# Squares of one gate group moved to the last quarter of the first gate/value phase

## The chip, the cores and the metric

The kernel runs on one core of one Trainium2 chip. The metric is the device time of one execution in microseconds, as the median of several runs. Its engines are TensorE (PE, with its weight loads as PEld), VectorE (DVE), ScalarE (ACT), GpSimd (POOL) and SyncE (SP). In this kernel SP only issues transfers; POOL issues transfers and a few small operations.

## The reference

A complex gated recurrence feeds a gated feed-forward block with a residual.

```
mag  = sqrt(a_re^2 + a_im^2);  scale = min(mag, 0.999) / (mag + 1e-6)
a    = (a_re + i a_im) * scale                       # 4 x 8 heads, 768 steps, 48 wide
S_t  = a_t * S_(t-1) + k_t v_t^T                     # complex state, real input
y_t  = q_t . Re(S_t)
x    = y as [3072 tokens, 384]
out  = x + sigmoid(x @ w_res) * ((gelu(x @ w_gate) * (x @ w_val)) @ w_out)
```

The widths are 384 for the model and 1536 for the feed-forward block.

## The kernel before, in words

**Groups and units.** The 768 steps of each of the four batches are cut in three stretches of 256. A batch and a stretch make a *group*: 256 tokens with all eight heads, held as two halves of 128 tokens on the partitions. There are 12 groups, ordered by stretch first. Groups are put together in *units*: group 0 alone, then 1 and 2, 3 and 4, 5 and 6, and so on, group 11 alone. So the fourth unit holds groups 5 and 6, and its first group is group 5. Group 6 is called `HELD`, and its squares are placed elsewhere in the program.

**How the recurrence becomes products.** For each group the log of the squared magnitude, `lm`, is summed along the tokens by products with a triangular matrix (`cs_l`, L272), and so is the angle `th` (`cs_t`, L291, reduced to a fraction of a turn on DVE in L295 and L296, with its absolute value in L301). Exponentials of the sums (`E`, `Ei`) and sines (`CS`) scale q and k (`products`, L369 to L381) into `padQ` and `padK`. Within a half the output is a masked score product times v; between halves and groups a decayed state `G` is carried. From group 3 on the transposed `QT` and `KT` come from a DMA transpose that SP issues (L385); the score products that read them are at L446. In earlier groups PE transposes (L459, L462) and ACT and DVE copy the result (`qk`, L464 and L465).

**The squares.** `squares(g)` gives three steps. `q0` (L217) squares `ar` on ACT into `lm`. `q1` squares `ai` on ACT into `sq` (L231; on DVE for groups 1 to 4). `q2` (L235) adds the two on DVE with a ceiling, and for groups 3 to 5 issues the decay transfers of that row on POOL (`decay_raw`, L333, then L316). The first two are allowed to go to the queue only after the last gelu issued so far (`paced("gelu")`), the third only after the last gelu product (`paced("gmul")`).

**Phases.** After a ramp, each unit `u` has a phase y (gate, value, gelu, their product, residual gate) and each following unit a phase x (logs, exponentials, angles, sines, and the output product of the unit before). Phase y of unit `u` takes in the first half of the attention of unit `u + 1`, the products of q and k for it, and the squares of a later unit. In phase y of unit 0 those are the three steps of group 5 alone. The gate/value work is twelve `gv_step`s (PE at L595 and L599, gelu on ACT, the product with the value on DVE at L602) and two residual gates (`rp_step`, PE at L611, a tanh on ACT, called `sg`). Their results share four PSUM banks with the transposes of x (`xt_step`, L580), so a product can wait for the bank that an earlier one frees. All calls of ACT's helper `act` show as L144; a change of ACT's function table is L639.

**What sets the order.** `weave` spreads the steps of each stream evenly between a begin and an end, and runs them in order of that place. A planner then puts the instructions of each engine in a queue; helpers such as `paced` and `tab` tie some of them down. [...] SP's queue holds the loads of `ar`, `ai`, `q` and `k` (L164, L172), the outputs (L626), one decay row per group (L349) and the DMA transposes (L385). POOL's queue holds the loads of v, the weights, the small decay transfers and the adding of residuals; a load of v waits on POOL until the `k` of the same group has landed (L201).

Of the kernel before, what the change touches and what calls it, by code (L numbers as in the profile page):

```python
# [17 lines left out]
def weave(*streams):  # L18

    order = []  # L20
    for si, (begin, end, steps) in enumerate(streams):
        n = len(steps)
        for i, step in enumerate(steps):
            order.append((begin + (end - begin) * (i + 0.5) / n, si, i, step))
    for _, _, _, step in sorted(order, key=lambda e: e[:3]):
        step()
# [3 lines left out]
def kernel(  # L30
# [36 lines left out]
    LATE0, LATE1 = 0.6, 1.0  # L67
# [141 lines left out]
    def paced(nm):  # L209
        return tc.issue_after(T[nm].ins) if nm in T else nullcontext()  # L210

    def squares(g):

        def q0():
            T["lm", g] = pS.tile([128, W], FP, tag="s", name="lm")
            with paced("gelu"):
                nc.scalar.activation(out=T["lm", g], in_=flat(T["ar", g]), func=AF.Square)  # L217

        def q1():
            if g < 5:  # L220
                if g == 0:
                    T["sq"] = hb.tile([128, 4, 2, DM], FP, tag="h2", name="sq0")
                t = T["sq"][:, g % 4].rearrange("p a m -> p (a m)")
            else:
                t = pE.tile([128, W], FP, tag="E", name="sq")
            T["sq", g] = t
            if g in DVSQ:
                nc.vector.tensor_tensor(out=t, in0=flat(T["ai", g]), in1=flat(T["ai", g]), op=OP.mult)
            else:
                with paced("gelu"):  # L230
                    nc.scalar.activation(out=t, in_=flat(T["ai", g]), func=AF.Square)  # L231

        def q2():
            with paced("gmul"):
                nc.vector._custom_dve(TENSOR_ADD_SAT, out=T["lm", g], in0=T["lm", g], in1=T["sq", g], s0=MAG2MAX, s1=0.0)  # L235
            if g in LATER and g != HELD:
                decay_raw(g)
        return [q0, q1, q2]
# [127 lines left out]
    def products(g):  # L366
        def x0():
            qE = flat(T["q", g]).bitcast(BF)[:, 0:W]
            nc.vector.tensor_tensor(out=qE, in0=flat(T["q", g]), in1=T["E", g], op=OP.mult)  # L369
            T["qE", g] = qE  # L370

        def x1():
            kE = flat(T["k", g]).bitcast(BF)[:, 0:W]
            nc.vector.tensor_tensor(out=kE, in0=flat(T["k", g]), in1=T["Ei", g], op=OP.mult)
            T["kE", g] = kE

        def mk(nm, src):
            def x():
                t = pads[nm, g % 2][:, :, 0:DD].rearrange("p x (u d) -> p x u d", u=2)
                sb = T[src, g].rearrange("p (x u d) -> p x u d", u=1, d=D).to_broadcast([128, C * H, 2, D])  # L380
                nc.vector.tensor_tensor(out=t, in0=T["CS", g], in1=sb, op=OP.mult)  # L381
                T[nm, g] = t
                if g >= TURN:
                    tt = trp.tile([128, C * H, 128], BF, tag=nm + "T", name=nm + "T")
                    T["turn"] = nc.sync.dma_start_transpose(out=tt, in_=pads[nm, g % 2])  # L385
                    T[nm + "T", g] = tt
            return x
        return [x0, mk("Q", "qE"), x1, mk("K", "kE")]
# [248 lines left out]
    def table(nm):  # L637
        def f():
            tab(nc.scalar.preload_act_table_set(nm))  # L639
        return f  # L640

    def gs(u):
        return UNITS[u] if 0 <= u < NU else []
# [7 lines left out]
    def call(f, *a):  # L651
        return lambda: f(*a)
# [4 lines left out]
    def att_steps(u, half):  # L657

        todo = [(g, c, i * C + c) for i, g in enumerate(gs(u)) for c in range(C)]
        n = len(todo) // 2  # L660
        steps = []
        for i, (g, c, jj) in enumerate(todo[half * n:half * n + n]):
            steps += attention(g, c)
            if i > 0:
                steps.insert(-1, call(xt_step, u, jj - 1))
        if n:
            steps.append(call(xt_step, u, half * n + n - 1))
        return steps
# [109 lines left out]
    def phase_y(u):  # L778

        gv = []  # L780
        if 0 <= u < NU:
            table("gelu_and_others")()
            gv = [call(gv_step, u, f) for f in range(KF)]
            rp = [call(rp_step, u, jj) for jj in range(len(gs(u)) * C)]
            gv = gv[:8] + rp[:len(rp) // 2] + gv[8:] + rp[len(rp) // 2:]
        def late(nm, f):
            with paced(nm):
                f()
        dec3 = [call(decay3, g) for g in gs(u + 1)]
        sq = [f for w in range(NU) if P1AT.get(w, w - 2) == u + 1 for g in gs(w) if g != HELD for f in squares(g)]  # L790
        pr = [(0.0, 0.4, [st for g in gs(u + 1) for st in products(g)])]
        if u == 0:
            g1, g2 = gs(1)
            pr = [(0.0, 0.15, [call(late, "last", f) for f in products(g1)]),
                  (0.35, 0.6, [call(late, "gmul", f) for f in products(g2)])]
        weave((0.0, 1.0, gv), *pr, (0.55, 0.56, dec3), (0.5, 0.95, sq), (0.3, 0.95, att_steps(u + 1, 0)) if u < 1 else (LATE0, LATE1, att_steps(u + 1, 0)))

    for g in range(3):
        load_a(g)
# [11 lines left out]
    for u in range(NU + 1):  # L811
        if u > 0:
            phase_x(u)
        if u == 1:
            with paced("turned"):
                decay_raw(HELD)
        residuals()
        phase_y(u)
        for g in gs(u + 2):
            with paced("turn"):  # L820
                load_q(g)
            after_landing(T["k", g], call(load_v, g))
        while T["a"] < min(NG, gs(u + 1)[-1] + 7 if gs(u + 1) else NG):
            with paced("turn"):
                load_a(T["a"])
# [30 lines left out]
```

## Time and profile before

| what | value |
|---|---|
| runs shown, median of 5 | 290.3 us (289.24 to 291.03) |
| profiled execution, time | 290.88 us |
| its span, first to last instruction | 288.9 us |
| granted TensorE clock, mean | 0.959 |
| PE busy | 244.5 us (85%) |
| DVE busy | 216.2 us (75%) |
| ACT busy | 198.4 us (69%) |
| POOL busy | 93.3 us (32%) |
| bytes moved | 44.01 MB, mean 152 GB/s |
| packets under 512 B | 165092 of 176001 |

The span is what the profile's views cover; the time of an execution has about 2 us more. Busy shares are means over the whole span: the phases differ in what limits them. Phase y of unit 0 covers about 43 to 68 us, phase x of unit 1 from there to about 91 us, and phase y of unit 1 from there to about 110 us, by the places of the table loads and gelus in the timeline of ACT.

### The profile page before, as it was taken

Reading aid. Unit: us, or ns where it says so; the run is one execution under the profiler, and the core shown is the slowest. Engines: PE = TensorE matmul, PEld = TensorE weight load, DVE = VectorE, ACT = ScalarE, POOL = GpSimd, SP = SyncE. Lnnn points to the kernel's source line nnn. Section 1 sums busy time; section 2 is a strip of 40 time slices with the busy share of each in tenths; the row PEclk is TensorE's granted clock in tenths of the full one; section 3 lists DMA queues with packets and bytes.
Section 4 is the critical chain, followed back from the end, with each engine's and each line's share of the span. In section 5 each row is a group of like instructions: output and inputs, shape, how many; then the busy total and the mean of one; then the engine's idle time right before and its main releaser. Section 6 shows DMA issues by size and latency. Waiting matters only on the chain.

```text
span 288.9 us, 5120 instructions
## 1 busy us (share of the span) xinstructions
PE 244.5 (85%) x1835; PEld 148.2 (51%) x1848; DVE 216.2 (75%) x376; ACT 198.4 (69%) x336; POOL 93.3 (32%) x141
## 2 busy tenths in 40 slices
PE   0445758866986998999999999989999998999994
PEld 0122437755653455554566554556545665455782
DVE  0679996945599986899796998869977577564553
ACT  4876996458798579995689975787565746455250
POOL 4021851130352602467304492124821242100220
PEclk9968987977899999999999999999999999999999
DMA  8999999899999999969999979997499566900631
GB/s 144 187 175 186 172 200 193 151 177 194 161 178 214 163 195 173 176 141 184 178 203 168 148 130 205 191 173 64 75 216 219 87 59 133 189 16 23 141 56 56
DMA packets 176001, 44.01 MB, mean 152 GB/s; under 512 B 165092, under 2 KB 175976, under 8 KB 175976
## 3 DMA queue, kind: packets, MB, share of 16 engines
q1 hardware_dynamic: 140744, 33.05, 67.1%
q0 software_dynamic: 35232, 10.64, 36.2%
q8 instruction: 14, 0.23, 0.3%
q14 instruction: 11, 0.09, 0.1%
HBM read 31.33 MB, written 9.08 MB: 140 GB/s over the span
## 4 chain that ended last, share of the span: by engine, by line
PE 61%; ACT 17%; DVE 8%; DMA 6%; issue 4%; SPq 3%; POOL 0%; DVEq 0%; ACTq 0%
PE vp L599 15%; PE gp L595 15%; PE op L619 12%; PE cst L291 4%; PE csl L272 3%; PE rp L611 3%; ACT L639 3%; DMA k<-in_k_dram 3%; ACT CS L144 2%; PE at L446 2%; ACT lm L144 2%; ACT ar L144 2%; DMA d<-lm 2%; SPq L172 2%; PE dk L488 2%
## 5 line engine op out<-in xcount | busy, mean ns | idle before, releaser
L144 ACT ACTIVATE h<-gp 128x512 bf16<-128x512 f32 (+1 forms) x84 | 44.7, 535 | 38.1 <-PE gp L595 37.9
L602 DVE SCALAR_TENSOR_TENSOR h<-h,vp 128x512 bf16<-128x512 bf16 (+1 forms) x84 | 50.6, 608 | 24.4 <-PE vp L599 15.2
L599 PE MATMUL vp<-xT,wv 128*128 128x512 bf16 (+1 forms) x252 | 62.6, 356 | 3.0 <-ACT sg L144 3.0
L595 PE MATMUL gp<-xT,wg 128*128 128x512 bf16 (+1 forms) x239 | 61.8, 354 | 3.3 <-ACT h L144 2.1
L619 PE MATMUL op<-wo,h 128*128 128x384 bf16 x288 | 50.9, 326 | 1.7 <-ACT xT L584 1.2
L599 PEld LDWEIGHTS <-wv 128*128 128x128 bf16 x252 | 25.0, 100 | 25.6 <-issue 3.3
L619 PEld LDWEIGHTS <-h 128*128 128x128 bf16 x288 | 27.3, 98 | 19.4 <-issue 3.2
L316 POOL DMA_DIRECT2D m<-d x32 | 22.4, 707 | 42.8 <-DMA d<-lm 15.6
L634 POOL DMA_DIRECT2D out_dram<-x x22 | 20.5, 950 | 46.3 <-DMA out_dram<-ot 42.8
L595 PEld LDWEIGHTS <-wg 128*128 128x128 bf16 x252 | 23.8, 100 | 20.1 <-issue 3.0
L449 DVE TENSOR_TENSOR atm<-at,mask 128x512 bf16<-128x512 f32 x36 | 24.6, 683 | 5.2 <-PE at L446 5.2
L639 ACT ACT_TABLE_LOAD x21 | 26.9, 1283 | 1.1 <-PEq L840 0.7
L178 POOL DMA_DIRECT2D v<-in_v_dram x24 | 21.7, 909 | 17.0 <-DMA ai<-in_a_im_dram 12.1
L272 PE MATMUL csl<-lm,lt0a 128*128 128x384 f32 x24 | 11.8, 578 | 13.1 <-ACT lm L144 11.9
L201 POOL COPY landed<-k 1x1 f32<-1x1 f32 x9 | 2.4, 268 | 58.0 <-DMA k<-in_k_dram 58.0
L622 DVE SCALAR_TENSOR_TENSOR ot<-sg,op 128x384 f32<-128x384 f32 x24 | 13.1, 547 | 8.4 <-PE op L619 7.0
L291 PE MATMUL cst<-ai,ut0b 128*128 128x384 f32 x40 | 17.4, 532 | 0.3 <-DVE ot L622 0.3
L144 ACT ACTIVATE ar<-ar 128x768 f32<-128x768 f32 x20 | 17.0, 855 | 0.1
L235 DVE CUSTOM_DVE_ANT_0 lm<-lm,sq 128x768 f32<-128x768 f32 x12 | 11.4, 950 | 7.3 <-ACT sq L231 7.3
L217 ACT ACTIVATE lm<-ar 128x768 f32<-128x768 f32 x12 | 10.0, 837 | 9.6 <-DMA ar<-in_a_re_dram 9.6
L144 ACT ACTIVATE sg<-rp 128x384 f32<-128x384 f32 x24 | 11.6, 489 | 7.2 <-PE rp L611 7.2
L501 ACT CAST x<-y 128x384 bf16<-128x384 f32 x22 | 10.5, 476 | 8.6 <-PE y L498 8.0
(113 smaller groups left out, 466.8 us busy)
## 6 DMA issues: line engine op xcount, KB each, us to landing
ar<-in_a_re_dram SPq DMA_DIRECT2D x24, 192.0 KB, 5.0
ai<-in_a_im_dram SPq DMA_DIRECT2D x24, 192.0 KB, 4.6
q<-in_q_dram SPq DMA_DIRECT2D x24, 192.0 KB, 5.1
k<-in_k_dram SPq DMA_DIRECT2D x24, 192.0 KB, 4.9
out_dram<-ot SPq DMA_DIRECT2D x24, 192.0 KB, 2.4
out_dram<-x POOLq DMA_DIRECT2D x22, 192.0 KB, 4.2
v<-in_v_dram POOLq DMA_DIRECT2D x24, 96.0 KB, 5.4
wg<-in_moe_w_gate_dram POOLq DMA_DIRECT2D x4, 288.0 KB, 7.3
```

The costliest lines, as they stand in the source:

```text
L144: return tab(nc.scalar.activation(**kw))
L178: held(nc.gpsimd.dma_start(out=t[:, c], in_=rows(v, g, c)), after)
L272: nc.tensor.matmul(out=cs, lhsT=lmat[c], rhs=T["lm", g][:, sl], start=True, stop=True)
L291: nc.tensor.matmul(out=cs, lhsT=tmat[c if s == 0 else 1], rhs=th[:, sl], start=True, stop=(s == 0 or c == 0))
L316: T["turned"] = nc.gpsimd.dma_start(out=m[u * D:(u + 1) * D].rearrange("p r h -> p (r h)"), in_=md.rearrange("r (h d) -> d (r h)", h=H))
L449: nc.vector.tensor_tensor(out=atm, in0=at, in1=mask4, op=OP.mult)
L595: nc.tensor.matmul(out=gp, lhsT=wg[:, fi, ffi * 128:(ffi + 1) * 128], rhs=xT[:, fi, :], start=(fi == 0), stop=(fi == KD - 1))
L599: nc.tensor.matmul(out=vp, lhsT=wv[:, fi, ffi * 128:(ffi + 1) * 128], rhs=xT[:, fi, :], start=(fi == 0), stop=(fi == KD - 1))
L602: T["gmul"] = nc.vector.scalar_tensor_tensor(out=h2[:, ffi, :], in0=h2[:, ffi, :], scalar=0.5, in1=vp, op0=OP.mult, op1=OP.mult)
L619: nc.tensor.matmul(out=ps, lhsT=h2[:, ffi, jj * 128:(jj + 1) * 128], rhs=wo[:, ffi, :], start=(ffi == 0), stop=(ffi == KF - 1))
L634: nc.gpsimd.dma_start(out=out[t0:t0 + 128, :], in_=x, accum_op=OP.add)
L639: tab(nc.scalar.preload_act_table_set(nm))
```

## The change

In phase y of unit 0 the stream of group 5's three square steps is spread between 0.75 and 1.0 of the phase, where it was between 0.5 and 0.95. With three steps the places go from 0.575, 0.725 and 0.875 to 0.792, 0.875 and 0.958. In the other phases the stream stays as it was.

```
@@ phase_y(u)
-        weave((0.0, 1.0, gv), *pr, (0.55, 0.56, dec3), (0.5, 0.95, sq), (0.3, 0.95, att_steps(u + 1, 0)) if u < 1 else (LATE0, LATE1, att_steps(u + 1, 0)))
+        weave((0.0, 1.0, gv), *pr, (0.55, 0.56, dec3), (0.75, 1.0, sq) if u == 0 else (0.5, 0.95, sq), (0.3, 0.95, att_steps(u + 1, 0)) if u < 1 else (LATE0, LATE1, att_steps(u + 1, 0)))
```

The planner answers with more than these three steps: in the queues of the built program the order also differs in places of the two phases after it, on PE, DVE and ACT, and in two places on POOL. SP's order is the same.

## The prediction

> **What bounds the kernel now.** I read the page's busy shares first (PE 85%, DVE 75%, ACT 69%), then the slices: PE is at 9 tenths nearly everywhere after 90 us and ragged before. So time won before 90 us is kept if PE meets no new wait. Next, the timelines of ACT and PE around 55 to 60 us, where the moved squares stand (columns: start, duration, engine, line, operation, idle before it and what ended that).
>
> ```profile
> 55.04 0.38 ACT L144 ACTIVATE h<-gp 128x256 bf16<-128x256 f32 x1 [0.27 <-PE gp L595]
> 58.66 0.84 ACT L217 ACTIVATE lm<-ar 128x768 f32<-128x768 f32 x1 [3.24 <-DMA ar<-in_a_re_dram]
> 59.41 0.47 ACT L144 ACTIVATE sg<-rp 128x384 f32<-128x384 f32 x1
> ```
> ```profile
> 59.93 0.49 PE L599 MATMUL vp<-xT,wv 128*128 128x256 bf16 x3 [2.99 <-ACT sg L144]
> ```
>
> The square of group 5 waits 3.24 us for its load. The gate's tanh is queued behind it, though its product was ready at 55.74 + 0.65 = 56.39; PE waits for the bank that the tanh frees, 2.99 us. Then I cut the stretches at the changes of the clock (stretch, length, busy us with counts of PE, weight loads, DVE, ACT and POOL, then PEclk, DMA share, GB/s):
>
> ```profile
> 57.54:60.96 3.42, 1.03 (x16) 0.94 (x16) 2.32 (x4) 2.05 (x4) 0.08 (x1) 1.00 0.78 155
> 60.96:64.37 3.41, 2.92 (x20) 2.06 (x19) 0.84 (x2) 1.81 (x5) 2.19 (x3) 0.50 1.29 186
> 64.37:67.78 3.41, 3.41 (x28) 2.70 (x27) 1.92 (x4) 1.59 (x3) 0.00 (x0) 0.50 1.27 195
> 67.78:71.20 3.42, 1.15 (x18) 0.87 (x16) 2.18 (x5) 3.19 (x5) 0.00 (x0) 1.00 1.27 184
> 71.20:74.61 3.41, 3.41 (x15) 2.39 (x16) 0.48 (x1) 2.25 (x6) 0.00 (x0) 0.50 1.28 212
> 88.26:91.68 3.42, 1.58 (x8) 0.59 (x7) 3.42 (x5) 3.31 (x4) 0.00 (x0) 1.00 1.63 218
> ```
>
> After a stretch with PE busy for 1.03 or 1.15 of 3.41 us the clock is 0.50 for 6.83 and 3.41 us; after 1.58 it stays 1.00. The stall therefore costs twice. Last, SP's queue and the first use of what it transposes:
>
> ```profile
> 86.32 1.19 SPq L626 DMA_DIRECT2D out_dram<-ot  x1
> 87.62 0.24 SPq L349 DMA_DIRECT2D d<-E  x1
> 88.37 0.35 SPq L626 DMA_DIRECT2D out_dram<-ot  x1
> 89.24 3.28 SPq L385 DMA_TRANSPOSE QT<-padQ  x1
> 92.64 3.17 SPq L385 DMA_TRANSPOSE KT<-padK  x1
> ```
> ```profile
> 100.91 0.39 PE L446 MATMUL at<-QT,KT 96*128 96x128 bf16 x4
> ```
>
> From 57.66 to 86.2 us SP issues loads without a pause, k of group 3 taking 7.5 us alone. KT lands 6.4 us after its issue, at 99.0, and is used at 100.91: slack 1.9 us. I distrust the page's chain between 58 and 82 us (SP, k, POOL, d<-lm, DVE lm L295): by the built program that L295 waits for the decay row of group 4, issued at 43.85, and DVE was busy up to it anyway.
>
> [...]
>
> **The change part by part.** Only three steps of group 5 move; no instruction is added or removed. In the built order of the changed kernel, ACT has behind the 55.04 gelu: tanh, gelu, x copy, gelu, square of ar, xT copy, gelu, square of ai, qk copy, last gelu, square of group 6 (before: behind that gelu too), qk copy, second tanh. SP's order is the same. On POOL the two m loads of group 5 go behind the v load of group 4.
>
> 1. *Stall.* Tanh at 56.4; PE goes on at 56.95 (its transposes end 56.56 + 0.39) instead of 59.93: 3.0 us.
> 2. *Clock.* Without that idle, 57.54 to 60.96 holds over 2 us of PE work, so the halved 6.83 us fall away: 6.33 us busy at half clock, worth 3.2.
> 3. *New waits in the phase.* The square of ar now stands at 58.4 and waits to 58.66; that of ai waits to 60.41 (landing, as before), with qk copy and last gelu behind it; group 6's waits for its ar, which lands 58.5 + 4.1 = 62.6, with 0.6 us of wait, a qk copy and the second tanh behind it. Walking ACT, PE and DVE with the row durations (gelu 0.38, square 0.84, qk copy 0.58, product 0.33 at full clock) I get the table load at 64.3 instead of 68.49, with one qk copy already done. Of the 6.2 us of steps 1 and 2 this phase keeps 4.2; landings take the rest.
> 4. *Next phase* (logs to sines, ACT and DVE bound). From the first Ln to the first gelu it is 70.27 to 91.32 = 21.05 us. Saved: qk copy 0.48, a wait of 1.13 for transposes at half clock, about 0.4 of a 1.02 wait for the saturated sum L235. Added: the k product now ahead of |f| of group 4, a 0.48 product behind it and a mask product earlier; DVE from L235 to that |f| is 9.48 - 0.6 - 0.48 + 0.87 = 9.27 us, no worse. First gelu at 84.8: 6.5 ahead.
> 5. *Where it stops.* PE would reach the scores L446 near 95 (100.91 - 6.5 and some slip). SP does not follow, since loads that nothing in the change touches hold it to 86.2. L626, L349 and L626 then need about 2.1 us, so QT starts at 88.3 (88.0 to 88.8; before it waited for padQ to 89.24), KT at 91.7, landing at 98.1. The scores come at 98.1: 2.8 us ahead, 2.6 taken for slip. The m2 loads behind SP's 87.62 row (POOL at 92.50, landing 2.9 to 4.7 later) allow the decay product by 98.5; it stood at 100.81, so it doesn't bind.
> 6. *Small.* Seven dk products (0.46 us) go ahead of the scores, into the new idle: 0.35. Decay loads of group 5 on POOL land by about 88 and are used past 107: nothing, and if late, Ln of that row waits.
>
> Sum against the profiled execution (290.88, span 288.9, so 2.0 around it): 290.88 - 2.6 - 0.35 = 287.9. It is 0.6 above the median 290.3; the end set by SP doesn't depend on that, so I take **288.0**, 2.3 below the median. What I can't see is the clock after the new idle, bounded at 0 and, for two windows at half, 3.4 us lost.
>
> **Rivals.**
> - *Clock falls at the new wait.* PE idles some 2 to 3.4 us before the scores at 98.1. [...] One or two windows at half clock cost 1.7 to 3.4 us, less what lies in the wait: 2.0. Time 289.9 (288.6 to 291.2). For it: 57.54 above. Against: a slower logs phase shortens the idle, and 1.58 busy did not trip it.
> - *Slower.* At the same place, if SP gets no further than now (scores 1.9 ahead at most, when KT lands) and the clock is half for two full windows of bound work up to 106: 290.3 + 3.4 - 1.9 = 291.8, with the 0.35 not won either. It decides from 1.45 + 1.9 = 3.35 us lost at half clock on. For: both waits now fall at one instruction. Against: padQ, which held QT to 89.24, comes five us earlier.
> - *No cap.* If SP's queue moves along with the engines (its loads waiting for buffers, as some rows name), all 6 us stay: 284.3. Against: the counts it waits for between 57 and 86 us belong to work done long before.
> - *It does nothing.* The next landings (60.41, 62.6) hold the tanh as ar did: 290. Against: only the second tanh is behind them.
>
> **How the numbers follow.** Main case 0.50 (287.0 to 288.8), clock case 0.30, slower 0.09, no cap 0.07, nothing 0.04. A measurement here tells about 0.5% (1.45 us) from no change: below 288.85 is faster, above 291.75 slower. Faster: 0.48 + 0.06 + 0.07 = 0.61, cut to 0.57, as the walk has many short steps and errors lie on the late side. Slower: 0.09 + 0.02 = 0.11. Same: 0.32. The range 286.4 to 291.1 leaves out no cap and the worst slower cases.
>
> **What would show it.** After: no ACT idle near 3 us ahead of a square at 58 us; PEclk 1.00 in 61 to 68; table load near 64.3; first 128x512 gelu near 85; QT's transpose at 88 to 89; PE idle ahead of L446 at about 98, ended by a DMA. Wrong, if the gelus start later than 88, if QT starts before 87, or if PEclk is 0.50 between 97 and 105.

## The result, and the profile after

The changed kernel takes 291.1 us (median; 289.33 to 294.64, 44 runs) and the kernel before 291.06 us (288.89 to 294.94, 79 runs) when they run beside each other. The ratio after to before is 1.0005, with a 95% interval of 0.9989 to 1.0022: no change. The profiled execution took 290.44 us (before 290.88), its span is 288.7 us (before 288.9). The ratios here are of the runs within 1.5% of a kernel's fastest, and since the profiled executions of late_after (294.26 us) and nowait_fast (293.75) lie outside that, I read from those two which wait follows which and places up to 110 us, and no time of the whole.

The table sets the loads of ACT's function table (L639) of the two profiled executions against each other. They mark the ends of the phases.

| start of | before, us | after, us | ahead, us |
|---|---|---|---|
| logs behind phase y of unit 0 | 68.49 | 63.85 | 4.64 |
| sines | 83.31 | 76.30 | 7.01 |
| gelus of phase y of unit 1 | 90.03 | 82.68 | 7.35 |
| logs behind it | 110.63 | 109.10 | 1.53 |
| gelus of unit 2 | 129.94 | 128.54 | 1.40 |
| gelus of unit 3 | 169.37 | 168.08 | 1.29 |
| logs behind it | 190.09 | 189.89 | 0.20 |
| last table load | 263.72 | 263.52 | 0.20 |

So in these two executions 7.35 us were won by 83 us, 5.8 of them were given back between 83 and 109 us, and one more between 168 and 190 us. How far the first of these differs from one execution to the next is taken up at steps 1 and 4 below.

The winning shows in ACT's timeline after (start, duration, engine, line, operation, idle before it and its releaser):

```profile
56.49 0.49 ACT L144 ACTIVATE sg<-rp 128x384 f32<-128x384 f32 x1 [1.01 <-PE rp L611]
...
58.42 0.85 ACT L217 ACTIVATE lm<-ar 128x768 f32<-128x768 f32 x1
...
62.14 0.84 ACT L217 ACTIVATE lm<-ar 128x768 f32<-128x768 f32 x1 [0.53 <-DMA ar<-in_a_re_dram]
...
63.85 1.28 ACT L639 ACT_TABLE_LOAD   x1
```

The tanh `sg` stands ahead of the square and runs at 56.49, where it ran at 59.41. The square of `ar` at 58.42 waits for nothing, since its load is there by now. The square of group 6 waits 0.53 us, and the table load comes at 63.85. The giving back shows in PE's timeline after:

```profile
57.03 0.49 PE L599 MATMUL vp<-xT,wv 128*128 128x256 bf16 x3
...
92.39 1.14 PE L611 MATMUL rp<-wr,xT 128*128 128x384 bf16 x6
98.56 0.61 PE L446 MATMUL at<-QT,KT 96*128 96x128 bf16 x4 [5.03 <-DMA KT<-padK]
...
180.66 0.40 PE L446 MATMUL at<-QT,KT 96*128 96x128 bf16 x4 [0.79 <-DMA KT<-padK]
```

The 2.99 us of idle ahead of the value product at 57.03 are gone. But PE has nothing left to do from 93.5 us on: the scores at 98.56 have waited 5.03 us for KT. Before, the same instruction waited for nothing, at 100.91: it is only 2.35 us ahead. A second wait for KT, 0.79 us at 180.66, takes most of the lead of 1.29 us: 0.20 is left. The list of waits after has the sum of them (total, times, longest):

```profile
PE at L446 <- DMA KT<-padK: 6.0, 3, 5.0
```

SP's timeline says why KT is not there:

```profile
62.89 8.66 SPq L172 DMA_DIRECT2D k<-in_k_dram  x2
...
86.73 1.20 SPq L626 DMA_DIRECT2D out_dram<-ot  x1
88.03 0.24 SPq L349 DMA_DIRECT2D d<-E  x1
88.80 0.35 SPq L626 DMA_DIRECT2D out_dram<-ot  x1
89.28 3.50 SPq L385 DMA_TRANSPOSE QT<-padQ  x1
92.89 3.38 SPq L385 DMA_TRANSPOSE KT<-padK  x1
```

SP stands in the same row of loads as before, 8.66 us in `k` of group 3 alone, and comes to the output at 86.73, where before it came there at 86.32. `padQ` was ready at 81.17 + 0.95 = 82.1; QT starts at 89.28, before at 89.24. KT, issued at 92.89, lands 5.6 us later, and the scores start at once. Last, the clock, in stretches cut at its changes (length, busy us with counts of PE, weight loads, DVE, ACT and POOL, PEclk, DMA share, GB/s):

```profile
94.54:97.95 3.41, 0.00 (x0) 0.00 (x0) 0.88 (x3) 0.22 (x1) 1.13 (x2) 0.99 1.11 221
97.95:101.36 3.41, 2.80 (x10) 1.31 (x11) 0.69 (x1) 0.88 (x2) 1.14 (x2) 0.51 0.85 142
101.36:104.77 3.41, 3.36 (x27) 1.62 (x26) 2.75 (x4) 2.33 (x6) 0.00 (x0) 1.00 1.20 245
```

The stretch from 94.54, in which PE was busy for 0.00 us, is followed by one at 0.51. This second one has 2.80 us of PE work in it. Three 128x512 products take 1.28 us there (98.96 to 100.24) and 0.65 us at full clock (101.64 to 102.29), so the stretch costs about 1.4 us (an estimate). The lead falls by only 0.8, from 2.35 at the scores to 1.53 at the next table load. Some work that stood behind the scores before, the `dk` products of step 6, is now done ahead of the wait.

### The profile page after: what moved, and what is told of

The parts are those of the page before. It is cut to its first block, busy times and chain, and to the rows that moved or that the text cites. A ratio compares the mean times of both kernels' runs of the same rounds, so it can differ in the third digit from the quotient of the medians.

```text
span 288.7 us, 5124 instructions
## 1 busy us (share of the span) xinstructions
PE 243.3 (84%) x1834; PEld 145.6 (50%) x1848; DVE 215.4 (75%) x376; ACT 198.4 (69%) x336; POOL 94.4 (33%) x141
## 2 busy tenths in 40 slices
DMA packets 176001, 44.01 MB, mean 152 GB/s; under 512 B 165092, under 2 KB 175976, under 8 KB 175976
## 4 chain that ended last, share of the span: by engine, by line
PE 55%; ACT 17%; DVE 12%; DMA 9%; issue 4%; SPq 2%; DVEq 0%; ACTq 0%
PE vp L599 11%; PE op L619 11%; PE gp L595 11%; DMA KT<-padK 8%; PE csl L272 5%; PE cst L291 4%; ACT L639 3%; PE rp L611 3%; PE at L446 2%; ACT lm L144 2%; ACT CS L144 2%; ACT ar L144 2%; PE dk L488 2%; PE y L496 1%; PE tpx L580 1%
## 5 line engine op out<-in xcount | busy, mean ns | idle before, releaser
L449 DVE TENSOR_TENSOR atm<-at,mask 128x512 bf16<-128x512 f32 x36 | 24.6, 684 | 8.0 <-PE at L446 7.9
L201 POOL COPY landed<-k 1x1 f32<-1x1 f32 x9 | 3.5, 387 | 60.7 <-DMA k<-in_k_dram 60.7
L446 PE MATMUL at<-QT,KT 96*128 96x128 bf16 x144 | 14.3, 221 | 6.5 <-DMA KT<-padK 6.0
L622 DVE SCALAR_TENSOR_TENSOR ot<-sg,op 128x384 f32<-128x384 f32 x24 | 13.2, 548 | 8.4 <-PE op L619 6.9
L446 PEld LDWEIGHTS <-KT 96*128 96x128 bf16 x144 | 10.4, 99 | 12.7 <-DMA KT<-padK 7.2
```

The source lines that it names most:

```text
L446: nc.tensor.matmul(out=at[:, j], lhsT=T["KT", g][0:DD, x0 + j], rhs=T["QT", g][0:DD, x0 + j], start=True, stop=True)
L449: nc.vector.tensor_tensor(out=atm, in0=at, in1=mask4, op=OP.mult)
```

## The experiments

Twelve kernels ran, in three sittings, each against the kernel before on the same chip. Those called fast, nowait or plain read other tokens' values in some places, so their output is not the reference's; they keep the amount of work.

| kernel | squares late (the change) | what else | ratio to before | 95% interval |
|---|---|---|---|---|
| after | yes | | 1.0005 | 0.9989 to 1.0022 |
| late_before | no | load of group 8 behind a KT | 1.003 | 1.0001 to 1.006 |
| late_after | yes | the same | 0.9943 | 0.991 to 0.9975 |
| fast_before | no | contiguous loads, groups 7 and 8 | 0.9975 | 0.9946 to 1.0004 |
| fast_after | yes | the same | 0.9887 | 0.9859 to 0.9915 |
| nowait_before | no | squares read older data | 0.9978 | 0.9956 to 1.0001 |
| nowait_fast | no | that, and contiguous loads | 0.9979 | 0.9946 to 1.0013 |
| nowait_fast_p | no | that, and POOL's order | 0.984 | 0.9801 to 0.9879 |
| late_m_before | no | late, and M behind two masks | 1.0111 | 1.0052 to 1.0171 |
| late_m_after | yes | the same | 0.9941 | 0.9917 to 0.9966 |
| late_p_after | yes | late, and POOL's order | 0.9904 | 0.9872 to 0.9935 |
| plain_before | no | contiguous loads, all later groups | 0.9913 | 0.9882 to 0.9945 |
| plain_after | yes | the same | 0.9819 | 0.9784 to 0.9853 |

### Is it SP's row of loads? (late, fast)

The theory: the loads that SP issues ahead of QT and KT hold the scores, whatever the gelus do. The first pair puts one of those loads, `ar` and `ai` of group 8, behind the KT of group 3. The second reads groups 7 and 8 with contiguous rows: their four pairs of loads take SP 1.36, 0.94, 0.88 and 0.87 us in fast_after, where they take 1.92, 3.47, 2.60 and 3.02 in after. In all kernels with changed loads, SP's queue as built also has its decay row (L349) ahead of the first output, where before and after have it behind; the order of PE, ACT and DVE is that of the kernel each is derived from, but for late_m. So the text on record for fast_after, that every order stays, holds but for that row.

```
 late:
-        while T["a"] < min(NG, gs(u + 1)[-1] + 7 if gs(u + 1) else NG):
+        while T["a"] < min(NG, gs(u + 1)[-1] + 7 - (u == 0) if gs(u + 1) else NG):
-                    T[nm + "T", g] = tt
+                    T[nm + "T", g] = tt; load_8(nm, g)
+    def load_8(nm, g):
+        if (nm, g) == ("K", 3):
+            with tc.issue_after(T["turn"].ins):
+                load_a(8)
 fast, in load_a:
-  in_=rows(src, g, c)
+  in_=(plain if g in (7, 8) else rows)(src, g, c)
+    def plain(a, g, c):
+        n = (g * C + c) * 128 * DM
+        return a.rearrange("b h s d -> (b h s d)")[n:n + 128 * DM].rearrange("(p h d) -> p h d", p=128, h=H)
```

> Theory (SP's queue): the change wins some 7 us by the first 128x512 gelu, and gives them back because the transposes of group 3 stand behind the loads of groups 7 and 8 on SP. With the load of group 8 behind KT of group 3, QT is issued when padQ is ready, near 82.3 us, KT lands near 92, PE idles under 1 us ahead of the scores L446, and the phase's next table load comes near 104 instead of 109.1. The kernel is 2 to 6 us faster than before, less what the later loads cost in the next unit. Rival (the gain is lost to the reordered queues or to the clock alone): within 1 us of before, as the changed kernel.

> The same move of the load of group 8 in the kernel before. Theory (SP's queue): QT can't be issued ahead of padQ, which is ready at 89.2 us here, so nothing is won at L446: within 1 us of before. Rival (the move of the load helps or hurts by itself): the same gain or loss as late_after shows, 2 us or more.

> The changed kernel with ar and ai of groups 7 and 8 read as contiguous rows of 1536 bytes (another part of the same tensors, so the values are not those of the tokens), which makes these eight loads cheap and leaves every order as it is. Theory (SP's queue): SP is past them by 80 us, QT is issued near 82.3, no wait of over 1 us at L446, 4 to 7 us faster than before. Rival (reordered queues or the clock): under 1.5 us faster.

> The kernel before with the same cheap loads of groups 7 and 8. Theory (SP's queue): QT still waits for padQ at 89.2 us, so at most 1 us is won. Rival (the loads are the bound whatever ACT does): 3 us or more faster, as fast_after.

Measured: the change is worth 0.9943 / 1.003 = 0.991 (0.987 to 0.996, the two half-widths added in quadrature) with the load moved, and 0.9887 / 0.9975 = 0.991 (0.987 to 0.995) with the cheaper loads; by the medians of all runs the two are 0.986 and 0.990. With the loads as they are it was worth nothing. late_before and fast_before stay within the 1 us that was expected of them. QT starts at 83.82 in late_after and at 83.50 in fast_after, instead of 89.28, and the first scores no longer wait. So SP's row is what held the gain back. The sizes fell short of what was expected: late_after is 0.57% or 1.7 us below before (2 to 6 expected), fast_after 1.13% or 3.3 us (4 to 7 expected), although its first scores, at 94.56, come some 6 us ahead of those of before. One reason is that the change wins less in these pairs: the first 128x512 gelu comes 3.2 us earlier in the late pair (88.04 and 84.84) and 3.9 us in the fast pair (89.03 and 85.17), not 7.3. Steps 1 and 4 below say why. The other is that something else is next in line.

### What is next in line (late_m)

PE's timeline of late_after shows it, with DVE's beside it:

```profile
94.23 0.39 PE L446 MATMUL at<-QT,KT 96*128 96x128 bf16 x4
...
99.39 0.58 PE L446 MATMUL at<-QT,KT 96*128 96x128 bf16 x4 [3.47 <-DVE atm L449]
```
```profile
97.78 0.16 DVE L361 TENSOR_TENSOR M<-m 96x8 f32<-96x8 f32 x1 [3.57 <-DMA m<-d]
```

The first scores come at 94.23 and wait for nothing. The second ones wait 3.47 us for the mask of the first (L449), which stands on DVE behind M, and M waits 3.57 us for the decay factor `m` that POOL fetches. In the changed kernel `m` was there at 96.22, ahead of KT, so that this wait did not show in the time. late_m takes M and the product with it out of the way:

```
-        return [hi(f) for f in (enter, grp(0), dk, grp(1), yy)]
+        return [hi(f) for f in ((grp(0), dk, grp(1), enter, yy) if (g, c) == (3, 0) else (enter, grp(0), dk, grp(1), yy))]
-  (0.55, 0.56, dec3)
+  (0.74, 0.74, dec3) if u == 1 else (0.55, 0.56, dec3)
```

> late_after, and on DVE the decay factor M of group 3 (L361, L362) and the product G<-G,M (L398) behind the first two score masks (L449) and the sum L235, where they stood ahead of the first; nothing is left out. In late_after the scores came at 94.23 without a wait for KT, DVE then stood 3.57 us for m and PE 3.47 us for DVE. Theory (that wait was the next one in line and takes back what late_after wins): PE idle ahead of the second scores under 1 us, no half clock between 96 and 104, the table load of the next phase at 104 to 106.5 us (late_after 108.36, after 109.10), 2 to 4 us less than late_after in that phase; some of it is lost again at the KT waits near 140 us, so the ratio is 0.984 to 0.993 against before. Rival (SP's transposes alone set the place, and the wait for m only stands beside it): 0.993 to 0.997, as late_after.

> The same two edits (load of group 8 behind the first KT transpose, M behind two score masks) on the kernel before. Theory: without the early gelus there is little to win there (late_before waited 1.68 us on PE for m): 1 to 2 us less than late_before, ratio 0.994 to 1.001 against before; the change is then worth 0.7 to 1.3% between this and late_m_after. Rival (the edits help by themselves, whatever the squares do): ratio under 0.992 here too.

Up to there it does what was expected: the second scores come at 96.97, the logs at 104.72, against 108.36. The time does not move: 0.9941, as late_after's 0.9943. From 104.72 to the next table load it takes 15.54 us, where late_after and after take 12.43 each, with the clock at a mean of 0.89. PE's timeline and SP's show what stands there:

```profile
106.74 0.40 PE L446 MATMUL at<-QT,KT 96*128 96x128 bf16 x4 [2.61 <-DMA KT<-padK]
```
```profile
93.24 3.08 SPq L164 DMA_DIRECT2D ai<-in_a_im_dram  x2
96.42 3.99 SPq L385 DMA_TRANSPOSE QT<-padQ  x1
100.50 3.31 SPq L385 DMA_TRANSPOSE KT<-padK  x1
```

This KT is that of group 4, the second of the same unit. The load of group 8, moved behind the KT of group 3, now stands ahead of it, and PE waits 2.61 us. In fast_after, where no load was moved, the KT of group 4 is issued at 94.17, lands 5.3 us later, and nothing waits for it. The stretch in which the wait lies (105.75 to 109.16, PE busy for 1.71 us in 36 short instructions) is followed by one at half clock. So the wait for `m` was next in line, as the theory had it, and behind it stands one that the moved load itself makes.

late_m_before was expected at 0.994 to 1.001 and came out at 1.0111, slower, with six runs: without the early gelus the same two edits do harm. Its profiled execution, the fastest of the six at 291.95 us, is 0.5 us ahead of before at the table load near 129 us and 0.9 us behind it at the one near 152 us; between them lies a wait of 0.95 us for KT (2.38 us in late_before), which before does not have. Why the other five took longer still, no trace shows.

### Is it the wait alone, or also the order? (nowait)

The change does two things: it moves the squares behind the landing of their load, and it changes the order of other instructions. nowait leaves the order of the kernel before and takes only the wait away.

```
-            nc.scalar.activation(out=T["lm", g], in_=flat(T["ar", g]), func=AF.Square)
+            nc.scalar.activation(out=T["lm", g], in_=flat(T["ar", 3 if g == 5 else g]), func=AF.Square)
 (q1 likewise, with "ai")
```

> The kernel before with one edit: group 5's two squares read the ar and ai of group 3, which landed long ago, so the decay values of group 5 are other numbers. Every queue keeps the order of the kernel before. Theory (the wait for the load is all that the change removes in the first gate phase, and the transposes queued on SP take it back): no ACT idle ahead of a square near 58 us, no half clock from 61 to 68, table load at 62.5 to 64.5 us, first 128x512 gelu at 82.5 to 85.5 (before 91.32), and then PE waits 3.5 to 6.5 us at L446 for KT; the time is the same as before within 0.5% (ratio 0.995 to 1.005). Rival (the new order of the instructions is what counts): the gelus come later than 87, or they come at 84 and PE does not wait for KT, and the ratio is under 0.992.

> The same edit together with the contiguous loads of ar and ai of groups 7 and 8 (values of other tokens), on the kernel before. Theory: as fast_after, since the wait is gone and SP is no longer late: ratio 0.984 to 0.992 against before (fast_after had 0.9887, fast_before 0.9975), the KT wait at L446 under 1 us. Rival (the new order is what counts): as fast_before, ratio 0.994 to 1.001.

ACT's timeline of nowait_before:

```profile
55.00 0.83 ACT L217 ACTIVATE lm<-ar 128x768 f32<-128x768 f32 x1
...
63.52 1.28 ACT L639 ACT_TABLE_LOAD   x1
```

The first phase ends at 63.52, as after: in that phase the wait is the whole of it. In the next phase it isn't. From the logs to the gelus' table nowait_before takes 85.06 - 63.52 = 21.54 us, exactly as before (90.03 - 68.49), and the changed kernel takes 82.68 - 63.85 = 18.83. The difference of 2.71 us is not the new order alone. nowait_fast has the order of nowait_before on PE, ACT and DVE, and takes 83.34 - 63.27 = 20.07. The clock tells the two apart (nowait_before, then nowait_fast):

```profile
63.11:66.53 3.42, 0.62 (x5) 0.46 (x6) 1.26 (x4) 3.39 (x6) 0.00 (x0) 1.00 1.24 185
66.53:69.94 3.41, 3.41 (x16) 2.26 (x15) 1.02 (x2) 2.56 (x7) 0.00 (x0) 0.50 1.27 184
```
```profile
63.27:83.34 20.07, 15.89 (x111) 9.66 (x113) 15.25 (x29) 18.73 (x32) 2.79 (x4) 1.00 1.22 216
```

With the old order this phase takes 20.06 or 20.07 us where the clock stays full (late_before, plain_before, nowait_fast) and 21.54 where one stretch of it is halved (before, fast_before, nowait_before); with the new order and full clock it takes 18.83 (after, late_after, fast_after). So at full clock the order is worth about 1.2 us, and the other 1.5 are a halved stretch that one execution meets and another does not. The new order does not rule it out: plain_after meets one (66.83 to 70.24) and takes 21.62. nowait_before meets another one at 87.01 to 90.42, among the gate products. So its first gelu, at 86.36, is later than I expected, and the wait for KT at 98.91 shorter, 1.30 us. The ratio, 0.9978, lies where the theory had it.

nowait_fast went against the theory: 0.9979, like fast_before, as its rival said. KT was no longer late (0.51 us), but POOL's timeline and DVE's show what was:

```profile
83.95 1.28 POOL L316 DMA_DIRECT2D m<-d  x2 [6.21 <-DMA d<-lm]
85.23 0.76 POOL L201 COPY landed<-k 1x1 f32<-1x1 f32 x1
85.94 1.79 POOL L178 DMA_DIRECT2D v<-in_v_dram  x2
87.71 0.53 POOL L345 DMA_DIRECT2D d<-Ei  x1
...
95.34 1.50 POOL L316 DMA_DIRECT2D m<-d  x2 [6.60 <-issue]
```
```profile
100.94 0.17 DVE L361 TENSOR_TENSOR M<-m 96x8 f32<-96x8 f32 x1 [6.73 <-DMA m<-d]
```

With the order of before, POOL waits 6.21 us to fetch the decay factor of group 5, then takes the v loads of group 4, and only then, at 87.71, issues `d<-Ei`, from which group 3's `m` is made. M comes at 100.94 after a wait of 6.73 us on DVE, and PE waited 5.65 us for it ahead of the second scores. In the changed kernel, where those fetches stand behind the v load, `d<-Ei` is at 83.47.

### POOL's order (p)

p moves nothing but these transfers; PE, DVE and ACT keep their order.

```
 in q2 of squares(g):
-            if g in LATER and g != HELD:
+            if g in LATER and g not in (5, HELD):
                 decay_raw(g)
 in the loop over the units, u == 1:
             with paced("turned"):
-                decay_raw(HELD)
+                decay_raw(5); decay_raw(HELD)
```

> nowait_fast with one more edit on POOL alone: the decay transfers of group 5 (L333 and two L316) go behind those that group 3's decay factor needs, where they stood ahead of them; PE, DVE and ACT keep their order. In nowait_fast POOL waited 6.2 us for them, issued d<-Ei at 87.71 (after: 83.47), and DVE then stood 6.73 us for m until 100.94. Theory (the place of these transfers on POOL, which the change also moves, is what made nowait_fast gain nothing): d<-Ei at 81 to 84, M at 93.5 to 97, PE idle ahead of the second scores 0 to 1.5 us, ratio 0.985 to 0.993 against before (nowait_fast 0.9979, fast_after 0.9887). Rival (m is late for another reason, or its wait only stands beside another): ratio 0.995 to 1.001.

> late_after with the same edit on POOL; nothing is left out. In late_after POOL waited 1.32 us for the transfers of group 5 ahead of d<-Ei (84.72), and DVE 3.57 us for m (until 97.78). Theory: d<-Ei at 82 to 83, M at 94.5 to 96, PE idle ahead of the second scores 0.5 to 2 us instead of 3.47, table load of the next phase 1.5 to 3 us earlier than in late_after (108.36); part of it is lost to KT near 140 us: ratio 0.988 to 0.995. Rival (later units set the end, and what is won before 105 us no longer counts, as in late_m_after): ratio 0.993 to 0.997, as late_after.

POOL's timeline of nowait_fast_p, and DVE's:

```profile
83.80 0.53 POOL L345 DMA_DIRECT2D d<-Ei  x1
...
90.27 1.50 POOL L316 DMA_DIRECT2D m<-d  x2 [5.44 <-DMA d<-Ei]
```
```profile
98.21 0.16 DVE L361 TENSOR_TENSOR M<-m 96x8 f32<-96x8 f32 x1
```

nowait_fast_p goes to 0.984 from nowait_fast's 0.9979: the place of three small transfers on POOL is worth 1.4% (0.986, 0.981 to 0.991, in quadrature over two sittings) once KT is on time. M ran a little later than I expected, at 98.21, but nothing waits for it there: the first scores themselves are at 98.31, since the phase ahead is 21.95 us long, with a stretch at half clock in it (68.02 to 71.43).

late_p_after has 0.9904, within what the theory had. In its trace `d<-Ei` is at 81.64, M at 95.04, the second scores at 96.66 without a wait, the logs at 104.48, 3.9 us ahead of late_after. KT is waited for in three places later on, 2.6 us in sum, and part of the lead goes there; the first and longest, 1.29 us at 105.16, is again for the KT of group 4 behind the moved load. Its time is below that of the kernel before in that sitting: 289.13 us against 291.97. Its interval overlaps late_after's, so that p's own share here (0.996, 0.991 to 1.001) isn't resolved.

### The later units (plain)

Here all loads of `ar` and `ai` from group 7 and of `q` and `k` from group 3 are contiguous, with the same function `plain`. All four inputs are float32, so rows of 192 bytes become rows of 1536; the 96 and 768 in the text on record are a slip.

> The changed kernel with all loads of ar and ai from group 7 and of q and k from group 3 contiguous (rows of 768 or 1536 bytes of other tokens instead of 96 or 192; the same bytes). Theory (SP's loads set both the place of the first KT and the KT waits near 140 and 180 us): k of group 3 takes under 3 us on SP (8.66), no KT wait over 0.5 us in any unit, and the lead of the early gelus is kept to the end but for the wait for m: 281 to 286.5 us, ratio 0.965 to 0.985 against before. Rival (the KT waits come from the transposes' own time, 3 to 5 us each on SP): KT waits of 1 to 3 us stay in the later units and the ratio is 0.985 to 0.99, as fast_after.

> The same loads on the kernel before. Theory: this kernel's stall is the landing of group 5's ar, which these loads follow, so it stays; QT follows padQ at once, and its ratio is 0.985 to 1.0 against before; the change is worth 0.8 to 1.6% between this and plain_after. Rival (SP's loads do not matter to what the change is worth): both ratios lie within 0.4% of each other.

SP's timeline of plain_after:

```profile
62.53 2.20 SPq L172 DMA_DIRECT2D k<-in_k_dram  x2
```

The same bytes of `k` that took SP 8.66 us take 2.20. No wait of PE for KT is left in any unit, as the theory had it. The contiguous rows also leave the DMA engines fewer packets (125825 instead of 176001), and the `v` load of group 4 comes earlier in POOL's order, so this pair alone does not tell SP's time from those two; late, with all its packets, does for the first unit. The change is worth 0.9819 / 0.9913 = 0.991 (0.986 to 0.995) again, within what was expected, and the time of plain_after, 286.9 us, is just outside (281 to 286.5).

## Why the prediction was wrong, step by step

- *1 Stall*, right for the execution it was read from: tanh at 56.49 (forecast 56.4), PE goes on at 57.03 (56.95). But the stall is not a fixed 2.99 us, as is shown behind this list.
- *2 Clock*, right in the same way: PEclk is 1.00 in every microsecond from 57 to 68.
- *3 New waits in the phase*, right: table load at 63.85 (64.3), 4.64 us ahead (4.2). nowait_before, with no wait for that load and the old order, gets to 63.52.
- *4 Next phase*, right and a little short: first 128x512 gelu at 83.98 (84.8), 7.3 us ahead (6.5). Of the 2.71 us won in this phase about 1.2 are the new order and 1.5 the halved stretch of before at 71.20, which not every execution has.
- *5 Where it stops* is the step that failed: the 2.6 us of lead that it carried from the scores to the end. Its mechanism was right, and late and fast show it: SP does not follow, and KT sets the scores. Three of its terms were off, all to the same side, and 0.20 us was left. First, QT started at 89.28 and not at 88.3, since SP came to the outputs 0.4 later than before and the half microsecond ahead of its second output stayed; the scores came 2.35 us ahead instead of 2.8. Second, the clock was taken at nothing. The gelus came a little earlier than forecast and KT later, so the idle grew from the 2 to 3.4 us that I had in mind to 5.03, long enough to leave one stretch of 3.41 us empty, and the next one ran at half clock, at a cost of about 1.4 us. PEclk at 0.50 between 97 and 105 was one of the forecast's own signs of being wrong, and it is what the trace shows. By the next table load the lead was 1.53. Third, the lead was carried to the end without another look at the later units. In the profile before, the first KT that phase y of unit 3 uses was issued at 172.89, landed 7.4 us later, at 180.3, and was used at 180.87: 0.6 us of slack. In the changed kernel it was issued 1.12 us earlier and took 8.8 us to land. There the lead fell from 1.29 to 0.20. That is one landing in one execution, and no run isolates it.
- *6 Small*: the 0.35 us of dk products can't be told apart in a lead of 0.20. The decay transfers of group 5, priced at nothing, cost nothing in this kernel. But with KT out of the way their place on POOL is worth 1.4%, and I had named their move without seeing that it is a gain waiting behind another. That `m` does not bind was right here (96.22, ahead of 98.56), and it is what binds next.

The stall of step 1 was read from one execution. late_before, fast_before, late_m_before and plain_before have the queues of before up to 60 us, and PE idles 2.70, 0.25, 0.38 and 0.91 us in its place, in fast_before so:

```profile
58.87 0.49 PE L599 MATMUL vp<-xT,wv 128*128 128x256 bf16 x3 [0.25 <-ACT sg L144]
```

In the last three the clock was halved until about 52 us (in before until 47.30), and the last gelu ahead of the square is at 56.72, 56.83 and 56.75 us (in before at 55.04). So ACT came to the square later and the load was nearly there: it waited 0.50, 0.63 and 1.16 us for it, in before 3.24. From table load to table load phase y of unit 0 takes 23.50 us in before, 20.86 to 22.38 in these four, and 18.50 to 19.89 in the six traces with the change: 3.0 us less by the two means, not 5.0. The forecast took the longest stall of five executions for that of the kernel.

The sum had 2.95 us; the two profiled executions differ by 290.88 - 290.44 = 0.44, and the medians do not differ. An execution of the kernel before with a shorter stall has less to win: in late_before, whose KT is early, the first scores come at 97.63, ahead of the 98.5 and 99.0 at which KT lands in after and before. So before, too, may wait for KT in such an execution, and that would be a part of why the change is worth nothing; no run shows it for before itself. The rival *Clock falls at the new wait* had a half clock behind that wait, as the trace has it (0.51), with a loss of 2.0 at the clock, and its weight of 0.30 was my estimate; it still carried 1.0 us to the end, which the later KT takes. *Slower* did not come about: its 3.35 us at half clock were 1.4. *No cap* needs other loads: plain_after, at 286.9 us, comes nearest to its 284.3, and only 2.7 us of that are the change's (plain_before has 289.61).

## What to carry to other kernels

Where a transfer queue sets the next meeting point, price the lead there and not where it is won. A lead is cut down to little more than the slack where the queue is held by other transfers: near 98 us SP did not come earlier (86.73, before 86.32), and 7.3 us became 2.35. It passes where the queue moves along: near 140 us before had 0.33 us of slack for KT, but the transposes came 1.3 us earlier too, and 1.2 us of lead were left. So ask at every later meeting point of the same kind which of the two it is. PE, early at a fixed point, did not only wait here; it also lost its clock (a stretch at 0.51 behind 5.03 us of idle, about 1.4 us by the estimate above). Waits for one place are stacked: take away the latest (KT) and the one behind it (`m`, 3.57 us in late_after) shows, so before pricing a fix, list the arrival times of all that meet there. A load that is moved out of the way stands in the way of what comes behind it, as in late_m (2.61 us for KT of group 4). And a wait that is read from one execution is one sample: the stall of 2.99 us was 0.25 to 2.70 in four others with the same order.

## What the runs showed of the hardware

- The clock: in after the stretch of 3.41 us with PE busy for 0.00 was followed by 3.41 us at 0.51 and then by 1.00. Of the stretches shown for the kernel before, those with 1.03 and 1.15 us of work (30 and 34%) were followed by one at 0.50, and the one with 1.58 by 1.00. Busy time alone does not tell which: in before the stretch from 37.06 has 1.88 us of it, in 27 short instructions, and the next one is at 0.50, while the one from 26.82 has 1.88 us in 19 and the next one is at 1.00. And the same order of instructions met a halved stretch in one execution and not in another (21.54 us and 20.07 us for the same phase in nowait_before and nowait_fast).
- What held SP: the two `k` loads of group 3, 192 KB each, took 8.66 us on SP with rows of 192 bytes and 2.20 us with contiguous rows. The same rows did not always take the same time: the two `k` loads of group 4, with rows of 192 bytes, took 1.87 us in the same trace (73.32). The row of eight pairs from `q` of group 3 on held SP for 25.9 us in after (60.69 to 86.61) and 15.1 us in plain_after (61.14 to 76.21). A DMA transpose held it between 1.3 and 5.7 us in after.
- A small decay row on POOL took two landings to arrive in nowait_fast: `d<-Ei` was issued at 87.71, the fetch of `m` followed at 95.34, and M at 100.94, so that 13.2 us lie between a 0.5 us instruction and the first one to use it.
